# Keys split by half of the partitions, chunk 0 laid out tile by tile, and a new order of chunk 1's start

## The chip, the cores and the metric

The kernel runs on one core of a Trainium2 chip. A core has a tensor engine for matrix products (PE), a vector engine (DVE), a scalar engine for activation functions (ACT), a general engine that here mostly issues loads (GpSimd, POOL in the profile) and a queue engine (SP). Each works through its own instructions in order, and semaphores tie them together. Products land in PSUM, eight banks of 2 KB for each of 128 partitions; everything else lies in SBUF. The metric is the time of one execution on the device in microseconds; less is better.

## What is computed

Causal attention over 4 batches, 8 heads, 768 positions and head width 64, in which three heads (0, 2, 6) look at all earlier positions and the other five only at the first 4 positions (the sinks) and at the last 64. Its result, as a matrix of 3072 by 512, goes through two dense layers with a leaky ReLU between them:

```python
scores = scale * np.matmul(q, k.transpose(0, 1, 3, 2))
stream_keep = causal & (is_sink | in_win)
mask = np.where(retr[0, :, 0, 0, None, None], full_mask, stream_mask)
...
a = a / (np.sum(a, axis=-1, keepdims=True) + 1e-09)
...
h = x @ w_in
g = np.maximum(0.01 * h, h)
return (g @ w_out).astype(np.float32)
```

with `w_in` of 512 by 2048 and `w_out` of 2048 by 512.

## The kernel before

The 3072 rows are cut into eight chunks of 384 (a half of one batch's positions), worked on in the order batch 0 first half, batch 1 first half, batch 0 second half, and so on. Chunk n's attention gives x for that chunk (`xts[n]`), then come the first layer in 16 ticks (`in_slots`, lines 547 to 557: four matmuls of 384 columns each, then ACT's leaky ReLU) and the second (`out_slots`). From chunk 2 on, keys and queries are transposed by DMA, and attention of the next chunk is woven slot by slot into the dense layers of the present one. The schedule is written by hand: every engine's order is the order in which the code issues instructions.

The change touches the start, where nothing is there to weave with. Names that matter:

- `kt[i]` holds the keys of one batch, transposed: head width along partitions, two heads in one group of 128 partitions. For each head of a pair there is a copy in which the other half of the partitions is zero (index `hh`), so that a product over 128 partitions gives one head's scores. `move` with `hh` writes such a copy out of PSUM by multiplying with a column of zeros and ones (`half`), lines 184 to 193.
- Chunk 0 is handled in three tiles of 128 positions (`First(0)`, `First(1)`, `First(2)`, lines 445 to 541). `turn_tile` (line 209) transposes a tile's keys or queries on PE into a bank with tag `py` and empties it: keys' even half by DVE ("v"), odd half by ACT ("a"); queries by DVE. `all_heads` (469), `retr` (480) and `stream` (493) put a mask into a bank by an identity product, add scores, and have ACT take the exponential. `av` (504) multiplies with values, `finish` (529) divides on DVE, and `x_t` (537) turns the result on PE and copies it into `xts[0]`.
- `v_shift_pe` (152) makes values shifted by 64 positions (`vb`) by a product and a DVE cast (line 160). The windowed heads of tiles 1 and 2 need them.
- `in_tile(q4, j)` (559) does four first-layer ticks for one tile of chunk 0: 16 matmuls of 128 columns and one ACT instruction. `q4` 0 needs the first 512 columns of `w_in`, `q4` 1 the second.
- `turn_pair` (195) transposes chunk 1's keys or queries for one pair of heads. `zero_small`, `sink_keys` and `sink_values` prepare the sinks of a batch.
- `Attention(1).slots(order, lag)` (409) gives chunk 1's attention as 12 units (scores and exponential), each followed `lag` slots later by its product with the values, and three further slots for turning x. Its buffers are six for full heads and five for windowed heads.
- PSUM banks: two each of the tags `ph`, `psS`, `po` and `py`.
- Loads with a change of type are issued by GpSimd in program order (lines 617 to 638), onto one queue.

At the end of the start, the order is (lines 707 to 737): first-layer pieces of the first weights with the keys of chunk 1, DVE memsets, first-layer pieces of the second weights, the queries of chunk 1, sinks of batch 1, then chunk 1's attention, into which the ticks 8 to 15 of chunk 0 (`p0[8:]`) are merged.

Of the kernel before, what the change touches and what calls it, by code (L numbers as in the profile page):

```python
# [11 lines left out]
FP32 = mybir.dt.float32  # L12
# [5 lines left out]
CH = 384  # L18
# [3 lines left out]
def kernel(  # L22
# [59 lines left out]
    kt = [bf(f"kt{i}", 4, 2, S) for i in range(2)]  # L82
# [82 lines left out]
    def zero_keys(i, eng, lo, hi):  # L165
        for hh in range(2):
            eng.memset(kt[i][64 - 64 * hh : 128 - 64 * hh, :, hh, lo:hi], 0.0)
# [8 lines left out]
    def q_of(n, p, lo, hi):  # L176
        if n < 2:
            return qx[n][:, p, lo:hi]
        g = lo // 128
        if hi <= 128 * g + 128:  # L180
            return qx[n][:, g, p, lo - 128 * g : hi - 128 * g]
        return qx[n][:, g : hi // 128, p, :]
# [12 lines left out]
    def turn_pair(n, p, tags, engs, nms="kq"):  # L195
        b, c = ORDER[n]
        if n not in qx:
            qx[n] = rot.tile([128, 4, CH], BF16, name="qt", tag="qt", bufs=2)
        for nm, tag, eng in zip(nms, tags, engs):
            pt = bank(tag, [128, 4, 128], BF16)  # L200
            for g in range(3):
                nc.tensor.transpose(pt[:, g, :], raw[nm, n][:, g, 2 * p : 2 * p + 2, :], ident[:])
            if nm == "k":
                for hh in range(2):
                    move(eng, kt[b % 2][:, p, hh, CH * c : CH * c + CH].rearrange("p (g t) -> p g t", g=3), pt[:, 0:3, :], hh)
            else:
                move(eng, qx[n][:, p, :].rearrange("p (g t) -> p g t", g=3), pt[:, 0:3, :])

    def turn_tile(nm, j, engs, tag="py"):
        pt = bank(tag, [128, 4, 128], BF16)  # L210
        for p in range(4):
            nc.tensor.transpose(pt[:, p, :], (k0 if nm == "k" else q0)[:, j, 2 * p : 2 * p + 2, :], ident[:])  # L212
        t = slice(128 * j, 128 * j + 128)
        if nm == "q":
            move(engs, qx[0][:, :, t], pt[:])
        else:
            for hh in range(2):
                move(engs[hh], kt[0][:, :, hh, t], pt[:], hh)
# [8 lines left out]
    def spreads(n):  # L227
        b, c = ORDER[n]

        def spread(g, hh):  # L230
            r = slice(64 * hh, 64 * hh + 64)
            o = CH * c + 128 * g
            nc.vector.tensor_copy(kt[b % 2][r, :, hh, o : o + 128], raw["kx", n][r, g])  # L233

        r = [lambda g=g, hh=hh: spread(g, hh) for g in range(3) for hh in range(2)]
        if c == 0:
            r += sink_keys_by(b)
        return r
# [14 lines left out]
    def sink_keys_by(b):  # L253

        ks, kk = ksink[b % 2], kt[b % 2]

        def odd():
            nc.vector.tensor_copy(ks[64:128, :].rearrange("p (q t) -> p q t", t=SK)[:, :, NS : 2 * NS],
                                  kk[64:128, :, 1, 0:NS])

        def even():
            nc.vector.tensor_copy(ks[0:64, 256 + 4 * NS : 256 + 5 * NS], kk[0:64, 2, 0, 0:NS])

        return [odd, even]
# [9 lines left out]
    class Attention:  # L274
# [35 lines left out]
        def retr(self, h):  # L310
            p, hh = divmod(h, 2)
            i, c, n = self.i, self.c, self.n
            groups = [[(0, 0)], [(1, 128), (2, 256)]] if c == 0 else \
                [[(kj, 0)] for kj in range(4)] + [[(4, 128), (5, 256)]]
            r = []
            for grp in groups:
                box = {}

                def qk(grp=grp, box=box):
                    s = self.score()  # L320
                    a = rot.tile([128, CH], BF16, name="at", tag="at", bufs=6)
                    off = 0
                    for j, (kj, lo) in enumerate(grp):
                        w = CH - lo
                        nc.tensor.matmul(  # L325
                            s[:, off : off + w], lhsT=kt[i][:, p, hh, 128 * kj : 128 * kj + 128],
                            rhs=q_of(n, p, lo, CH), start=(j == 0), stop=(j == len(grp) - 1),
                            skip_group_check=True)
                        off += w
                    nc.scalar.activation(out=a[:, 0:off], in_=s[:, 0:off], func=ACTF.Exp, scale=SM)  # L330
                    if len(grp) == 2:
                        d = a.rearrange("p (j t) -> p j t", j=3)[:, 0:3:2, :]
                        nc.vector.tensor_mul(d, d, m_caus.rearrange("p (o t) -> p o t", o=1).to_broadcast([128, 2, 128]))  # L333
                    elif grp[0][0] >= 3 * c:
                        nc.vector.tensor_mul(a[:, 0:128], a[:, 0:128], m_caus[:])  # L335
                    box[0] = a

                def do_av(grp=grp, box=box):
                    off = 0
                    for (kj, lo) in grp:  # L340
                        for qi in range(lo // 128, 3):
                            o = off + 128 * qi - lo
                            self.av(p, hh, qi, box[0][:, o : o + 128], va[self.b][:, kj, h, :])
                        off += CH - lo

                r.append((qk, do_av, p))
            return r

        def stream(self, h):
# [4 lines left out]
            def qk():  # L354
# [3 lines left out]
                for m in range(6):  # L358
                    k0 = 64 * max(6 * c + m - 1, 0)
                    nc.tensor.matmul(  # L360
                        s[:, 64 * m : 64 * m + 64], lhsT=kt[i][:, p, hh, k0 : k0 + 128],
# [83 lines left out]
    class First:  # L445
        def __init__(self, j):
            self.j = j
            self.at_of, self.po, self.xs = {}, {}, {}
# [7 lines left out]
        def key(self, h, k0):  # L456
            return kt[0][:, h // 2, h % 2, k0 : k0 + 128]

        def query(self, h, lo=0, n=128):
            return qx[0][:, h // 2, 128 * self.j + lo : 128 * self.j + lo + n]  # L460
# [8 lines left out]
        def all_heads(self, half, tag):  # L469
            hs = (RETR + STREAM)[4 * half : 4 * half + 4]  # L470
            s = self.bank_with(tag, over(n_first, 4), 4) if half else bank(tag, [128, 4, 128], FP32)
            if not half:
                for x, m in ((slice(0, 3), over(n_caus, 3)), (slice(3, 4), over(n_first, 1))):
                    nc.tensor.matmul(s[:, x, :], lhsT=ident[:], rhs=m, start=(x.start == 0), stop=False, skip_group_check=True)
            for x, h in enumerate(hs):
                nc.tensor.matmul(s[:, x, :], lhsT=self.key(h, 0), rhs=self.query(h), start=False, stop=True,
                                 skip_group_check=True)
            nc.scalar.activation(out=self.at[:, 4 * half : 4 * half + 4, :], in_=s[:], func=ACTF.Exp, scale=SM)

        def retr(self, lo, hi, tag):  # L480
            s = self.bank_with(tag, over(n_caus, 3), 0 if lo else 3)
            for x, blk in enumerate(self.blocks[lo:hi]):
                if blk is None:
                    for p in range(4):
                        nc.tensor.matmul(s[:, x, :], lhsT=ksink[0][:, 128 * p : 128 * p + 128],
                                         rhs=qx[0][:, p, self.qs], start=(x == 0 and p == 0), stop=(p == 3),
# [17 lines left out]
        def av(self, half):  # L504
# [9 lines left out]
            for h in sorted(hs, key=lambda h: h not in RETR):  # L514
                x = h - 4 * half
                if j == 0:
                    mm(x, x + 1, self.at[:, (RETR + STREAM).index(h), :], va[0][:, 0, h, :])
# [19 lines left out]
        def x_t(self, tag, eng):  # L537
# [3 lines left out]
            move(eng, xts[0][:, :, self.qs], pt[:])  # L541
# [5 lines left out]
    def in_slots(n, tags=("ph",)):  # L547
        def tick(t):
# [3 lines left out]
            for g in range(KG):  # L552
                nc.tensor.matmul(ph[:, 0:CH], lhsT=w_in_bf[:, g, 128 * t : 128 * t + 128],  # L553
                                 rhs=xts[n][:, g, :], start=(g == 0), stop=(g == KG - 1))
# [4 lines left out]
    def in_tile(q4, j, tag="ph"):  # L559
# [3 lines left out]
        for x in range(4):  # L563
            t = 4 * q4 + x
            for g in range(KG):
                nc.tensor.matmul(ph[:, x, :], lhsT=w_in_bf[:, g, 128 * t : 128 * t + 128],  # L566
                                 rhs=xts[0][:, g, 128 * j : 128 * j + 128], start=(x == 0 and g == 0),
# [60 lines left out]
    load_qk(1, "k")  # L628
    load_in(512, 1024)
    load_qk(1, "q")  # L630
# [35 lines left out]
    qx[0] = rot.tile([128, 4, CH], BF16, name="qt", tag="qt", bufs=2)  # L666
    xts[0] = rot.tile([128, 4, CH], BF16, name="xt", tag="xt", bufs=2)
    F0, F1, F2 = (First(j) for j in range(3))
    idle("psS", 13)
    turn_tile("k", 0, "va")  # L670
    turn_tile("q", 0, "v")
    sink_values(0, nc.vector)
    nc.vector.tensor_copy(vs[0][0:32, :, D], m_sink[0:32, :])
    turn_tile("k", 1, "va")
    F0.all_heads(0, "psS")
    F0.all_heads(1, "ph")
    turn_tile("q", 1, "v")
    sink_keys(0)
    F1.retr(0, 4, "psS")
    F1.stream((1, 3, 4, 5), ats4[0], "ph")  # L680
    F0.av(0)
    F0.finish(0)
    turn_tile("k", 2, "va")
    F0.av(1)
    F1.retr(4, 7, "psS")
    F1.stream((7,), ats[0], "ph")
    turn_tile("q", 2, "v")
    F0.finish(1)
    v_shift_pe(0, "py", "v")
    F2.retr(0, 4, "psS")  # L690
    F2.retr(4, 8, "ph")
    F0.x_t("py", "v")
    F1.av(0)
    F1.finish(0)
    F2.stream((1, 3, 4, 5), ats4[1], "psS")
    nc.vector.memset(ats[1][:, :, 1:3, :], 0.0)
    F1.av(1)
    F1.finish(1)
    F2.retr(8, 10, "ph")
    F2.stream((7,), ats[1], "psS")  # L700
    v_shift_pe(1, "py", "v")
    F1.x_t("py", "a")
# [3 lines left out]
    F2.finish(1)  # L706
    in_tile(0, 0)
    in_tile(0, 1)
    F2.x_t("py", "v")
    turn_pair(1, 0, ("psS",), "v", "k")  # L710
    turn_pair(1, 1, ("psS",), "v", "k")
    in_tile(0, 2)
    turn_pair(1, 2, ("psS",), "v", "k")
    turn_pair(1, 3, ("py",), "v", "k")
# [4 lines left out]
    in_tile(1, 0)  # L719
    in_tile(1, 1)  # L720
    in_tile(1, 2)
# [5 lines left out]
    a1 = Attention(1, po_tags=("po", "po", "po", "py"), xt_eng="v").slots([0, 2, 6, 1, 3, 4, 5, 7], lag=4)  # L727
    sink_keys(1)
    sink_values(1, nc.vector)
    nc.vector.tensor_copy(vs[1][0:32, :, D], m_sink[0:32, :])  # L730


    run(a1[0:8])
    v_shift_pe(0, "ph", "v", 1)
    run(a1[8:9])
    v_shift_pe(1, "ph", "v", 1)
    run(a1[9:10], merge(p0[8:], a1[10:]))
# [76 lines left out]
```

## Time and profile before

| | |
|---|---|
| median of 13 runs | 239.71 us (238.51 to 242.73) |
| profiled execution | 238.64 us, of which the span from first to last instruction is 236.9 us |
| instructions | 5040 |
| granted clock of the tensor engine, mean | 1.0 |
| chunk 0's tiles, from the first turn (5.3 us) to the first-layer work (16.9 us) | 11.6 us |
| from there to chunk 1's first score (24.3 us) | 7.4 us |
| from there to the first tick of chunk 1's first layer (about 37.25 us) | 13.0 us |
| the rest | 199.6 us |

The page of the profile gives busy time by engine, the chain of work that ended last, and groups of instructions. The timeline lists instructions in order of time: start, duration, engine, line, operation, what is written from what, shape, and in brackets how long the engine had been idle and what released it. A row with "x6" merges six neighbours. The row of a matmul includes the time that the product takes to come out of the array, so neighbouring rows overlap; how far apart matmuls start is read from the next row's start. A transfer's "landing" counts from its issue.

### The profile page before, as it was taken

The page shows a single profiled execution, that of the slowest core. Times are in us where ns is not written, and L with a number is a line of the kernel's source. Part 1 is how long each engine was busy: PE and PEld are TensorE (multiplying, and loading weights), DVE is VectorE, ACT ScalarE, POOL GpSimd, SP SyncE. Part 2 cuts the span into 40 slices and gives each one's busy share as a digit, 9 for nine tenths or more (in the row PEclk, how much of TensorE's full clock was granted, in tenths as well). Part 3 has the DMA queues.
Part 4 walks back from the last instruction along what each step waited for, and adds up shares of the span by engine and source line. Part 5 has one row for each costly group of instructions (what it writes and reads, how often), then busy time and mean ns, then how long its engine had stood idle before and what let it go on. Part 6 is the DMA issues. An engine that isn't in the chain of part 4 may idle for free.

```text
span 236.9 us, 5040 instructions
## 1 busy us (share of the span) xinstructions
PE 225.1 (95%) x2029; PEld 139.2 (59%) x2057; DVE 98.6 (42%) x280; ACT 128.1 (54%) x276; POOL 69.9 (30%) x85
## 2 busy tenths in 40 slices
PE   5889899999999999999999999999999999999994
PEld 3679565545565666566556565666556665555553
DVE  6687777025356266446413651156212341111121
ACT  4565866623754888564356544765556763333300
POOL 8986525029075059009403900000000000000000
PEclk9999999999999999999999999999999999999999
DMA  9999999999999949999999992920210221111112
GB/s 129 159 184 163 206 207 163 177 113 173 168 248 203 215 79 134 167 134 122 142 131 193 160 146 61 225 75 17 78 47 0 64 69 26 47 44 44 47 44 90
DMA packets 109352, 28.98 MB, mean 122 GB/s; under 512 B 101264, under 2 KB 105616, under 8 KB 109328
## 3 DMA queue, kind: packets, MB, share of 16 engines
q0 software_dynamic: 77024, 13.37, 75.2%
q1 hardware_dynamic: 31248, 15.01, 29.1%
q10 hardware_dynamic: 1056, 0.26, 0.5%
q8 instruction: 16, 0.26, 0.4%
q14 instruction: 8, 0.07, 0.1%
HBM read 27.30 MB, written 6.29 MB: 142 GB/s over the span
## 4 chain that ended last, share of the span: by engine, by line
PE 87%; DVE 5%; ACT 3%; issue 2%; DMA 2%; POOL 0%; POOLq 0%; DVEq 0%
PE ph L553 32%; PE py L579 28%; PE po L294 6%; PE psS L325 5%; PE psS L579 4%; PE psS L360 2%; PE ph L566 2%; PE psS L305 2%; DMA out_dram<-o 2%; ACT ats L365 1%; PE psS L403 1%; PE py L212 1%; ACT at L330 1%; DVE xs L393 1%; PE po L510 1%
## 5 line engine op out<-in xcount | busy, mean ns | idle before, releaser
L553 PE MATMUL ph<-xt,w_in_bf 128*128 128x384 bf16 x480 | 95.5, 326 | 0.1
L555 ACT ACTIVATE g<-ph 128x384 bf16<-128x384 f32 x120 | 58.9, 491 | 57.8 <-PE ph L553 57.3
L579 PE MATMUL py<-w_out_bf,g 128*128 128x512 bf16 (+1 forms) x324 | 85.5, 374 | 1.4
L553 PEld LDWEIGHTS <-w_in_bf 128*128 128x128 bf16 x480 | 43.7, 97 | 31.3 <-issue 1.2
L579 PEld LDWEIGHTS <-g 128*128 128x128 bf16 x400 | 35.4, 97 | 25.9
L330 ACT ACTIVATE at<-psS 128x384 bf16<-128x384 f32 x78 | 36.9, 490 | 15.5 <-PE psS L325 15.3
L585 DVE COPY o<-py 128x512 f32<-128x512 f32 (+1 forms) x22 | 14.9, 678 | 51.8 <-PE py L579 50.4
L112 POOL DMA_DIRECT2D kb<-in_k_dram x21 | 18.7, 908 | 32.0 <-DMA kd<-kb 31.3
L325 PE MATMUL psS<-qd,kt 128*128 128x384 bf16 (+2 forms) x90 | 22.9, 293 | 0.0
L117 POOL DMA_DIRECT2D va<-in_v_dram x24 | 21.3, 911 | 2.5 <-DMA w_out_bf<-in_moe_w_out_dram 1.7
L112 POOL DMA_DIRECT2D qb<-in_q_dram x21 | 18.7, 917 | 4.7 <-DMA w_in_bf<-in_moe_w_in_dram 1.8
L294 PE MATMUL po<-va,at 128*128 128x65 bf16 x228 | 19.4, 193 | 0.3 <-DVE at L333 0.3
L365 ACT ACTIVATE ats<-psS 128x384 bf16<-128x384 f32 x35 | 17.0, 489 | 4.6 <-PE psS L360 4.2
L369 DVE TENSOR_TENSOR ats<-ats,m_win 128x384 bf16<-128x384 bf16 x35 | 13.0, 374 | 14.8 <-ACT ats L365 14.7
L294 PEld LDWEIGHTS <-at 128*128 128x128 bf16 x234 | 15.1, 98 | 5.6 <-DVE at L333 0.7
L393 DVE TENSOR_TENSOR xs<-po,linv 128x384 bf16<-128x384 f32 x27 | 15.1, 558 | 0.9
L335 DVE TENSOR_TENSOR at<-at,m_caus 128x128 bf16<-128x128 bf16 x21 | 4.7, 225 | 24.2 <-ACT at L330 24.1
L233 DVE COPY kt<-kd 64x512 bf16<-64x512 bf16 x36 | 14.4, 399 | 0.6
L360 PEld LDWEIGHTS <-kt 128*128 128x128 bf16 x210 | 10.8, 98 | 6.3 <-issue 0.4
L325 PEld LDWEIGHTS <-kt 128*128 128x128 bf16 x99 | 9.5, 97 | 7.7 <-issue 1.2
L294 PEld LDWEIGHTS <-ats 128*128 128x128 bf16 x210 | 10.0, 97 | 4.4 <-DVE ats L369 1.1
L333 DVE TENSOR_TENSOR at<-at,m_caus 128x256 bf16<-128x256 bf16 x21 | 6.1, 291 | 14.1 <-ACT at L330 14.1
(136 smaller groups left out, 192.8 us busy)
## 6 DMA issues: line engine op xcount, KB each, us to landing
out_dram<-o SPq DMA_DIRECT2D x23, 256.0 KB, 2.3
va<-in_v_dram POOLq DMA_DIRECT2D x24, 128.0 KB, 6.8
kb<-in_k_dram POOLq DMA_DIRECT2D x21, 128.0 KB, 5.5
qb<-in_q_dram POOLq DMA_DIRECT2D x21, 128.0 KB, 5.7
w_in_bf<-in_moe_w_in_dram POOLq DMA_DIRECT2D x4, 512.0 KB, 9.4
w_out_bf<-in_moe_w_out_dram POOLq DMA_DIRECT2D x4, 512.0 KB, 12.5
vb<-va SPq DMA_DIRECT2D x8, 195.0 KB, 4.0
vb<-va SPq DMA_DIRECT2D x4, 130.0 KB, 3.4
```

Source lines behind the costliest of these rows:

```text
L112: nc.gpsimd.dma_start(out=t[:, g], in_=nat[nm][b, c, :, :, g])
L117: nc.gpsimd.dma_start(out=va[b][:, 3 * c + g, :, 0:D], in_=nat["v"][b, c, :, :, g])
L294: nc.tensor.matmul(o, lhsT=lhsT, rhs=rhs, start=first, stop=False, skip_group_check=True)
L325: nc.tensor.matmul(s[:, off : off + w], lhsT=kt[i][:, p, hh, 128 * kj : 128 * kj + 128], rhs=q_of(n, p, lo, CH), start=(j == 0), stop=(j = ...
L330: nc.scalar.activation(out=a[:, 0:off], in_=s[:, 0:off], func=ACTF.Exp, scale=SM)
L360: nc.tensor.matmul(s[:, 64 * m : 64 * m + 64], lhsT=kt[i][:, p, hh, k0 : k0 + 128], rhs=q_of(n, p, 64 * m, 64 * m + 64), start=(m == 0), s ...
L365: nc.scalar.activation(out=av_, in_=s[:, 0:CH].rearrange("p (j e f) -> p j e f", j=3, e=2), func=ACTF.Exp, scale=SM)
L393: nc.vector.tensor_tensor(xs[:], po[:, :, :, 0:D], linv.to_broadcast([128, 3, 2, D]), op=ALU.mult)
L553: nc.tensor.matmul(ph[:, 0:CH], lhsT=w_in_bf[:, g, 128 * t : 128 * t + 128], rhs=xts[n][:, g, :], start=(g == 0), stop=(g == KG - 1))
L555: nc.scalar.activation(out=gs[n][:, t, :], in_=ph[:, 0:CH], func=ACTF.Prelu, alpha=0.01)
L579: nc.tensor.matmul(py[n][:, 0 : c1 - c0], lhsT=gs[n][:, ng, 128 * tt : 128 * tt + 128], rhs=w_out_bf[:, ng, c0:c1], start=(ng == 0), stop= ...
L585: nc.vector.tensor_copy(o[:, 0 : c1 - c0], py[n][:, 0 : c1 - c0])
```

## The change

Keys lie in one SBUF tile for each half of the partitions (`kt[i][hh]`), not in one tile with an index for it. Chunk 0's queries and x lie tile behind tile (`[128, 3, 4, 128]`), so each tile is written as one run, and the first layer reads x in three runs of 128. `turn_tile` is taken apart into `turn` (PE) and `empty` (DVE or ACT), and `all_heads` into `masked`, `all_heads` and `weigh`; the two groups of four heads in tile 0 become even heads (0, 2, 6, 4) and odd heads. `turn_pair` takes an engine for each half of the keys, DVE and ACT for chunk 1 where both were DVE. GpSimd issues chunk 1's queries ahead of the second 512 columns of `w_in`. The order of the start is rewritten, and in chunk 1 the products with values follow six slots behind their scores, not four.

```diff
-    kt = [bf(f"kt{i}", 4, 2, S) for i in range(2)]
+    kt = [[bf(f"kt{i}_{hh}", 4, S) for hh in range(2)] for i in range(2)]
...
-    def turn_tile(nm, j, engs, tag="py"):
-        pt = bank(tag, [128, 4, 128], BF16)
+    turned = {}
+
+    def turn(nm, j, tag="py"):
+        pt = turned[nm, j] = bank(tag, [128, 4, 128], BF16)
         for p in range(4):
             nc.tensor.transpose(pt[:, p, :], (k0 if nm == "k" else q0)[:, j, 2 * p : 2 * p + 2, :], ident[:])
-        t = slice(128 * j, 128 * j + 128)
+
+    def empty(nm, j, engs, hh=None):
+        pt = turned[nm, j]
         if nm == "q":
-            move(engs, qx[0][:, :, t], pt[:])
-        else:
-            for hh in range(2):
-                move(engs[hh], kt[0][:, :, hh, t], pt[:], hh)
+            move(engs, qx[0][:, j], pt[:])
+        for h, eng in zip(range(2) if hh is None else (hh,), engs if nm == "k" else ""):
+            move(eng, kt[0][h][:, :, 128 * j : 128 * j + 128], pt[:], h)
...
+        HEADS = (0, 2, 6, 4, 1, 3, 5, 7)
+
+        def masked(self, half, tag):
+            s = self.s[half] = self.bank_with(tag, over(n_first, 4), 4) if half else bank(tag, [128, 4, 128], FP32)
             if not half:
                 for x, m in ((slice(0, 3), over(n_caus, 3)), (slice(3, 4), over(n_first, 1))):
                     nc.tensor.matmul(s[:, x, :], lhsT=ident[:], rhs=m, start=(x.start == 0), stop=False, skip_group_check=True)
+
+        def all_heads(self, half):
+            hs, s = self.HEADS[4 * half : 4 * half + 4], self.s[half]
             for x, h in enumerate(hs):
                 nc.tensor.matmul(s[:, x, :], lhsT=self.key(h, 0), rhs=self.query(h), start=False, stop=True,
                                  skip_group_check=True)
-            nc.scalar.activation(out=self.at[:, 4 * half : 4 * half + 4, :], in_=s[:], func=ACTF.Exp, scale=SM)
+
+        def weigh(self, half):
+            nc.scalar.activation(out=self.at[:, 4 * half : 4 * half + 4, :], in_=self.s[half][:], func=ACTF.Exp, scale=SM)
...
-    load_qk(1, "k")
+    load_qk(1)
     load_in(512, 1024)
-    load_qk(1, "q")
     load_v(1)
...
     idle("psS", 13)
-    turn_tile("k", 0, "va")
-    turn_tile("q", 0, "v")
+    turn("k", 0)
+    empty("k", 0, "va")
+    turn("q", 0)
+    empty("q", 0, "v")
+    F0.masked(0, "psS")
+    F0.masked(1, "ph")
     sink_values(0, nc.vector)
+    turn("k", 1)
+    F0.all_heads(0)
+    F0.all_heads(1)
+    F0.weigh(0)
+    empty("k", 1, "va")
+    turn("q", 1)
+    empty("q", 1, "v")
+    F0.weigh(1)
+    sink_keys(0)
     nc.vector.tensor_copy(vs[0][0:32, :, D], m_sink[0:32, :])
-    turn_tile("k", 1, "va")
-    F0.all_heads(0, "psS")
-    F0.all_heads(1, "ph")
-    turn_tile("q", 1, "v")
-    sink_keys(0)
     F1.retr(0, 4, "psS")
     F1.stream((1, 3, 4, 5), ats4[0], "ph")
+    F1.retr(4, 7, "psS")
     F0.av(0)
+    turn("k", 2)
+    empty("k", 2, "v", 0)
     F0.finish(0)
-    turn_tile("k", 2, "va")
     F0.av(1)
-    F1.retr(4, 7, "psS")
+    empty("k", 2, "a", 1)
     F1.stream((7,), ats[0], "ph")
-    turn_tile("q", 2, "v")
+    turn("q", 2)
+    empty("q", 2, "v")
+    v_shift_pe(0, "py", "v")
     F0.finish(1)
-    v_shift_pe(0, "py", "v")
     F2.retr(0, 4, "psS")
     F2.retr(4, 8, "ph")
-    F0.x_t("py", "v")
     F1.av(0)
     F1.finish(0)
     F2.stream((1, 3, 4, 5), ats4[1], "psS")
+    F2.retr(8, 10, "ph")
+    F1.av(1)
+    F0.x_t("py", "v")
+    F1.finish(1)
     nc.vector.memset(ats[1][:, :, 1:3, :], 0.0)
-    F1.av(1)
-    F1.finish(1)
-    F2.retr(8, 10, "ph")
     F2.stream((7,), ats[1], "psS")
     v_shift_pe(1, "py", "v")
-    F1.x_t("py", "a")
     F2.av(0)
     F2.finish(0)
     F2.av(1)
     F2.finish(1)
+    F1.x_t("py", "a")
     in_tile(0, 0)
     in_tile(0, 1)
     F2.x_t("py", "v")
-    turn_pair(1, 0, ("psS",), "v", "k")
-    turn_pair(1, 1, ("psS",), "v", "k")
+    turn_pair(1, 0, ("psS",), ("va",), "k")
+    turn_pair(1, 1, ("psS",), ("va",), "k")
     in_tile(0, 2)
-    turn_pair(1, 2, ("psS",), "v", "k")
-    turn_pair(1, 3, ("py",), "v", "k")
+    turn_pair(1, 2, ("psS",), ("va",), "k")
+    turn_pair(1, 3, ("py",), ("va",), "k")
     nc.vector.tensor_copy(m_win0[:, 2:], m_one.rearrange("p (o t) -> p o t", o=1).to_broadcast([128, 4, 64]))
     zero_small(1, nc.vector)
     for a in ats[2:]:
         nc.vector.memset(a[:, :, 1:3, :], 0.0)
-    in_tile(1, 0)
-    in_tile(1, 1)
-    in_tile(1, 2)
+    sink_keys(1)
+    sink_values(1, nc.vector)
+    nc.vector.tensor_copy(vs[1][0:32, :, D], m_sink[0:32, :])
     turn_pair(1, 0, ("psS",), "v", "q")
     turn_pair(1, 1, ("py",), "a", "q")
     turn_pair(1, 2, ("psS",), "v", "q")
     turn_pair(1, 3, ("py",), "a", "q")
     p0 = in_slots(0)
-    a1 = Attention(1, po_tags=("po", "po", "po", "py"), xt_eng="v").slots([0, 2, 6, 1, 3, 4, 5, 7], lag=4)
-    sink_keys(1)
-    sink_values(1, nc.vector)
-    nc.vector.tensor_copy(vs[1][0:32, :, D], m_sink[0:32, :])
-
-
-    run(a1[0:8])
+    a1 = Attention(1, po_tags=("po", "po", "po", "py"), xt_eng="v").slots([0, 2, 6, 1, 3, 4, 5, 7], lag=6)
+
+
+    run(a1[0:3])
+    in_tile(1, 0)
+    run(a1[3:5])
+    in_tile(1, 1)
+    run(a1[5:6])
+    in_tile(1, 2)
+    run(a1[6:7])
     v_shift_pe(0, "ph", "v", 1)
-    run(a1[8:9])
+    run(a1[7:8])
     v_shift_pe(1, "ph", "v", 1)
-    run(a1[9:10], merge(p0[8:], a1[10:]))
+    run(a1[8:9], merge(p0[8:], a1[9:]))
```

## The prediction

> **What bounds the kernel now.** I read the page first (busy time, then the chain), then the waits, then the timeline of the first 38 us, where every edited line lies. On the page, the busy row (us, share of the span, instructions) and the chain's shares by engine:
>
> ```profile
> PE 225.1 (95%) x2029; PEld 139.2 (59%) x2057; DVE 98.6 (42%) x280; ACT 128.1 (54%) x276; POOL 69.9 (30%) x85
> ...
> PE 87%; DVE 5%; ACT 3%; issue 2%; DMA 2%; POOL 0%; POOLq 0%; DVEq 0%
> ```
>
> The tensor engine (PE) is the bound. After 38 us its waits that the profile names come to 1.2 us, so a shift made before 38 us goes through to the end almost whole. What can move is the start: chunk 0's tiles up to 16.9 us, then its first weights and chunk 1's turning up to 24.3, then chunk 1's attention. In the last of these (start:end, length, PE busy) the row is
>
> ```profile
> 24.28:37.25 12.97, 11.95 (x148) 1.00 1.32 202
> ```
>
> where PE has slack that busy time hides, since a matmul's row includes its pipeline. By start-to-start spacing (128 columns 0.056 us, 384 columns 0.163, 256 columns 0.109, 64 or 65 columns 0.03, two of 455 in 0.38) the content is: six score groups 0.98, sinks 0.44, 30 stream scores 0.84, 48 products with values 1.44, sink products 0.27, shifted values 0.77, 12 turns of x 0.67, eight first-layer ticks 8 x 0.65 = 5.2; together 10.6 of 12.97 us. So 2.4 us are open, 2.0 of them before the first tick at 29.73.
>
> **The start, part by part.** *Separate key tiles.* Among the waits between 5 and 25 us (total, times, longest) stands
>
> ```profile
> ACT kt L193 <- DVE kt L189: 2.2, 3, 1.0
> ```
>
> ScalarE (ACT) empties the odd half only when VectorE (DVE) has done the even one. Is the shared tile the reason, or the shared bank of PSUM? Two rows speak against the tile: DVE and ACT write chunk 1's query tile from two banks at once (DVE from 23.87 to 24.56, ACT from 24.19), and PE reads keys of tile 0 at 7.82 while DVE writes tile 1's until 8.11. The Trainium skill (PSUM — Partial Sum Buffer, "PSUM bank collisions raise a hardware error") speaks against this edit as well: two engines must be kept off one bank, two readers included. So I cost the split at zero. By the other reading all three waits would go; carried through the steps below, only 0.25 us of it reaches chunk 1, since DVE is late there anyway.
>
> *Masks ahead, even heads first.* Keys and queries of tile 0 are turned by 6.3; the masks' 1024 columns go out at the slow early rate (four 128-column matmuls in 0.43, in place of 0.22 after 9 us), 0.86 us, then tile 1's keys 0.43: first scores at 7.64, before 7.82. Tile 1's queries are then emptied at 9.20, before 9.41. Gain 0.2.
>
> *Tile 2's keys in two steps.* Shifted values need a bank ("py"). Turned at 10.78, the even half leaves on DVE at 11.21 (0.46 us). The odd half queues on ACT behind three exponentials (10.09, 10.57, 11.05) and waits for DVE: 11.74 to 12.43. The other bank holds tile 2's queries, on DVE behind the even keys and F0's division (0.55): free at 12.64. So the shift starts at 12.47, before 12.38: the gain is gone.
>
> *F0's x moved back.* These are DVE's rows around it before (start, duration, instruction):
>
> ```profile
> 13.80 0.42 DVE L187 COPY xt<-py 128x512 bf16<-128x512 bf16 x1 [0.20 <-PE py L540]
> 14.14 0.17 DVE L532 RECIPROCAL linv<-po 128x4 f32<-128x4 f32 x1
> 14.35 0.42 DVE L534 TENSOR_TENSOR xs<-po,linv 128x256 bf16<-128x256 f32 x1
> 14.76 0.22 DVE L696 MEMSET ats<- 128x192 uint32 x1
> 14.89 0.17 DVE L532 RECIPROCAL linv<-po 128x4 f32<-128x4 f32 x1
> 15.10 0.43 DVE L534 TENSOR_TENSOR xs<-po,linv 128x256 bf16<-128x256 f32 x1
> 15.66 0.63 DVE L160 CAST vb<-py 128x455 bf16<-128x455 f32 x1
> ```
>
> The copy filled a gap at 13.80. Now it comes after F1's second product: PE turns x at 14.94, DVE copies at 15.37 (0.34 to the next), then division 0.55 and memset 0.2, and the cast of shifted values, on which F2's products wait, starts at 16.47 in place of 15.66: 0.8 later. F1's x is no longer turned inside that wait but after it, 4 x 0.056 = 0.22. Chunk 0's first-layer work then starts at 17.9, before 16.89: **+1.0**. Not shown in any row is how the engines fall into step in the new order. Ends: -0.2 if the copy finds a gap again, +1.3 if each stall is paid in full; I take +1.0, the rows above it in sequence.
>
> **Chunk 1's queries.** Before, DVE's queue there was:
>
> ```profile
> 19.10 0.42 DVE L187 COPY xt<-py 128x512 bf16<-128x512 bf16 x1 [1.18 <-PE py L540]
> 19.44 2.16 DVE L189 TENSOR_SCALAR kt<-psS,half 128x384 bf16<-128x384 bf16 x6
> 21.51 0.73 DVE L189 TENSOR_SCALAR kt<-py,half 128x384 bf16<-128x384 bf16 x2
> 22.16 0.22 DVE L715 COPY m_win<-m_one 128x256 bf16<-128x256 bf16 x1
> 22.38 0.28 DVE L170 MEMSET ksink<- 128x272 uint32 x1
> 22.73 0.49 DVE L171 MEMSET vs<- 128x520 bf16 x1
> 23.21 0.63 DVE L718 MEMSET ats<- 128x192 uint32 x3
> 23.87 0.69 DVE L187 COPY qt<-psS 128x384 bf16<-128x384 bf16 x2
> 24.59 0.58 DVE L258 COPY ksink<-kt 64x16 bf16<-64x16 bf16 x1
> 25.19 0.16 DVE L262 COPY ksink<-kt 64x4 bf16<-64x4 bf16 x1
> 25.26 0.61 DVE L127 TENSOR_TENSOR vs<-vsf,m_sink 32x448 bf16<-32x448 f32 x1
> 25.80 0.28 DVE L730 COPY vs<-m_sink 32x8 bf16<-32x8 bf16 x1
> ```
>
> It is full from 19.10 to 26. PE spent 20.82 to 23.5 on the second weights (48 matmuls, 2.69 us), which covered this list; the queries' copy at 23.87 came just as they were turned. The change takes that cover away and moves the last four rows ahead of the queries. Anew, from x at 19.10 + 1.0 = 20.1: x 0.34, two even key halves 0.72, to 21.17. The other two wait until PE, which may begin the third tile of the first weights only after x (20.58, 0.9 us), has turned keys again: 21.85, to 22.57. Window mask and memsets, 22.16 to 23.87 before: 1.71, to 24.28. Sink keys and values 1.5, to 25.75. First query copy 0.35; **first score at 26.15, before 24.28: +1.85, of it 0.85 from here**. ACT takes the four odd halves; of 128x384 with a scale there is no row, the nearest are ACT's plain copy (0.44) and its 128x512 with scale (0.69). I take 0.5: done by 23.4, under DVE's list; at 0.69 by 24.2, still under it. Ends for this part: 0.5 if DVE's small rows shrink (sink keys took 0.28 the first time, 0.58 here), 1.1.
>
> *Transfers.* GpSimd issued the second weights at 10.91 (landing 9.1 us later) and chunk 1's queries from 11.65 (9.1 each). Exchanged, the queries land some 2.7 us sooner, near 19.9, and the weights near 22.6 (2.7 is the time from chunk 1's last keys, 17.3, to these weights, 20.0). Needed at 22.0 and 27.2: nothing waits, nothing is gained, because DVE's list decides. At their old place, 20.8, these weights would cost 1.8. What GpSimd issues next (values, third weights) keeps its place; SP issues nothing in the moved steps.
>
> **Chunk 1's attention** now holds 10.6 + 2.7 = 13.3 us of content. The weight pieces fill part of the 2.0 us that waited for exponentials; the first scores still wait for banks and ACT. I leave 0.9 us open: 14.2, before 12.97: **+1.2**. Ends: +0.7 (only the 0.35 behind 29.73 stays open) and +2.7 (nothing filled). Lag 6 only lets products wait longer; the six score buffers and five stream buffers are just enough. The matmul that reads x with a stride of 512 has a near row: chunk 2's scores read queries so, at 0.33 us like the others: zero.
>
> **Sum:** 1.0 + 0.85 + 1.2 = 3.05. The profiled execution took 238.64 (span 236.9), so 241.7 by its own time. It was among the quickest; the median is 239.71, and I carry the same 3.0 there: **242.7 us**. Ends: 239.71 + (-0.2 + 0.5 + 0.7) = 240.7, and + 5.1 = 244.8.
>
> **Rivals.** *Clock drop, slower still.* Between 21.8 and 26.15 PE would have only 12 transposes, 0.67 us of work. The skill (TensorE: Matmul & The Clock Gate, "HAM oscillation — how this bites in real kernels") says that an idle window of about 3.4 us halves the clock. In this trace no pause after 9 us is longer than 0.6, so no row shows it; what half rate costs, its first 9 us show (four turns in 0.61, later 0.39). By the row: nothing. By the rule: some 3.4 us at half rate lose 1.7: 244.4. Whether turns count as work is open; chance 0.25.
> *Faster: DVE's list ends early.* It is four key halves shorter (1.44 us), and the start may tighten more than I think. If the first query copy came at 21.6, right behind its turn, the score would follow at 22.0, and 22.0 + 14.2 = 36.2 against 37.25: 238.7. It decides below 23.0 for the first score; above, the 14.2 eats it. Against it: five groups of rows stand ahead of that copy in DVE's order. Chance 0.12.
> *No change:* the start gains 0.8 in place of losing 1.0 and attention loses only 0.7: 239.71 - 0.8 + 0.85 + 0.7 = 240.4, near the edge of no change. Chance 0.07, shared by same and slower.
>
> **The numbers.** My forecast has 0.56. About 0.3% (0.7 us) is what a measurement of this kernel can tell from no change. Faster 0.12, same 0.05, slower 0.83. Range 240.7 to 245.0: both ends of the sum and the clock drop are inside, the fast case and most of the even one are out, under 2 in 10.
>
> **What would show it.** ACT's odd keys still 0.04 behind DVE's; the cast of shifted values for F2 near 16.5; DVE's first copy of chunk 1's queries near 25.7, with PE nearly empty for 4 us ahead; the last turn of chunk 1's x followed by chunk 1's ticks near 40.2. Wrong if that copy comes before 23, if odd and even keys overlap, or if weight matmuls after the pause run at 0.11 us each.

## The result, and the profile after

The changed kernel takes **242.81 us**, median of 11 runs (241.37 to 243.0); the kernel before, run on the same chips, 239.89 us (48 runs). The ratio is 1.0106, with a 95% interval of 1.0082 to 1.0129: slower by 2.9 us. The forecast was 242.7. Its sum is right and its composition is not: a cost that it put at nothing was made good by others that it had too large, so part of the hit is luck. The rest of this text is about the difference. Runs named e1 to e12 are the experiments below.

The profiled execution took 241.56 us (span 239.8). The 11 times fall into two groups, four near 241.5 and seven from 242.3 to 243.0; the profile is of the first, and what parts the two is open. From its page, the busy row, the granted TensorE clock in 40 slices, and the chain's shares by engine:

```profile
PE 225.1 (94%) x2029; PEld 139.5 (58%) x2057; DVE 96.4 (40%) x276; ACT 129.7 (54%) x280; POOL 70.0 (29%) x85
...
PEclk9999799999999999999999999999999999999999
...
PE 88%; DVE 3%; ACT 3%; DMA 2%; issue 1%; ACTq 0%; DVEq 0%
```

PE is as busy as before to the tenth, 225.1 us, in a span that is 2.9 longer. The one digit that differs from a 9 is the fifth slice, 24 to 30 us: there the clock was cut. The windows of that stretch (start:end length, then PE, PEld, DVE, ACT, POOL busy, clock, DMA share, GB/s) cover chunk 1's key and query turning, the first 7.9 us of its attention, and the rest of it:

```profile
20.78:24.42 3.64, 1.15 (x13) 0.79 (x12) 3.55 (x14) 2.27 (x5) 1.29 (x3) 1.00 2.05 174
24.42:32.28 7.86, 7.54 (x96) 6.39 (x96) 2.68 (x10) 5.22 (x12) 3.97 (x5) 0.78 1.24 205
32.28:40.17 7.89, 7.89 (x106) 5.45 (x103) 5.99 (x19) 4.83 (x11) 3.64 (x5) 1.00 1.83 181
```

For 3.64 us PE worked 1.15, and DVE 3.55. Then comes a stretch at a mean clock of 0.78; the trace's own record has half rate from 24.98 to 28.39, 3.41 us long. What PE waited for up to 41 us, the costliest first (total, times, longest):

```profile
PE psS L328 <- DVE qt L187: 1.9, 1, 1.9
PE py L214 <- DVE k L671: 1.3, 1, 1.3
PE po L519 <- DVE vb L160: 1.1, 1, 1.1
PE py L156 <- ACT kt L193: 0.6, 1, 0.6
```

The first is new: chunk 1's first score waits 1.9 us for DVE to copy the queries. This is DVE's queue ahead of that copy (start, duration, instruction):

```profile
18.89 0.42 DVE L187 COPY xt<-py 128x512 bf16<-128x512 bf16 x1 [1.40 <-PE py L549]
19.23 0.73 DVE L189 TENSOR_SCALAR kt<-psS,half 128x384 bf16<-128x384 bf16 x2
20.67 0.42 DVE L189 TENSOR_SCALAR kt<-psS,half 128x384 bf16<-128x384 bf16 x1 [0.71 <-PE psS L202]
...
21.33 0.22 DVE L734 COPY m_win<-m_one 128x256 bf16<-128x256 bf16 x1
...
23.02 0.31 DVE L261 COPY ksink<-kt 64x16 bf16<-64x16 bf16 x1
23.35 0.16 DVE L265 COPY ksink<-kt 64x4 bf16<-64x4 bf16 x1
23.42 0.61 DVE L127 TENSOR_TENSOR vs<-vsf,m_sink 32x448 bf16<-32x448 f32 x1
23.96 0.17 DVE L740 COPY vs<-m_sink 32x8 bf16<-32x8 bf16 x1
24.03 0.60 DVE L187 COPY qt<-psS 128x384 bf16<-128x384 bf16 x2
```

The queries had been turned by 22.6; mask and memsets hold DVE until 23.02, and from there to 24.03 the sinks' four rows alone hold the copy. And PE's rows from there on:

```profile
22.23 0.33 PE L202 MATMUL py<-ident,qb 128*128 128x128 bf16 x3
24.42 0.59 PE L328 MATMUL psS<-qt,kt 128*128 128x384 bf16 x3 [1.87 <-DVE qt L187]
25.32 0.48 PE L328 MATMUL psS<-qt,kt 128*128 128x384 bf16 x1 [0.31 <-ACT at L333]
25.60 1.91 PE L575 MATMUL ph<-xt,w_in_bf 128*128 128x128 bf16 x16
27.30 0.84 PE L328 MATMUL psS<-qt,kt 128*128 128x256 bf16 x3
27.95 1.27 PE L575 MATMUL ph<-xt,w_in_bf 128*128 128x128 bf16 x16
```

The first weight piece takes 1.70 us from start to start (25.60 to 27.30), 0.106 a matmul; 16 such matmuls at full clock take 0.9, as the first experiment below shows.

To see where the time arises, three points of each profile are enough: the start of chunk 0's first-layer work, chunk 1's first score, and the start of the ticks behind chunk 1's last turn of x ("last ticks"). A column "later by" gives the time since the point to its left. From the last point to the end it is 200.3 us in the kernel before and after, and within 0.3 of it in most experiments, so what is lost up to it is what is lost. The last column belongs to the start: PE's clock is half in the first microseconds and rises at a time that differs from execution to execution.

| kernel (profile) | first-layer work | first score | later by | last ticks | later by | full clock from |
|---|---|---|---|---|---|---|
| before | 16.89 | 24.28 | 7.39 | 36.60 | 12.32 | 8.86 |
| after | 16.68 | 24.42 | 7.74 | 39.53 | 15.11 | 4.50 |
| e1, pause filled | 17.98 | 25.58 | 7.60 | 39.22 | 13.64 | 9.90 |
| e3, weights back | 17.43 | 25.17 | 7.74 | 37.56 | 12.39 | 8.21 |
| e9, queries first | 17.73 | 23.44 | 5.71 | 37.32 | 13.88 | 8.82 |
| e11, before with a longer warm-up | 16.01 | 23.39 | 7.38 | 35.72 | 12.33 | 6.84 |

Between the two kernels nearly the whole loss lies in chunk 1's attention, 15.11 against 12.32.

### The profile page after: what moved, and what is told of

Read it like the earlier page. It is cut to its first block, busy times and chain, and to the rows that moved or that the text cites. A ratio compares the mean times of both kernels' runs of the same rounds, so it can differ in the third digit from the quotient of the medians.

```text
span 239.8 us, 5042 instructions
## 1 busy us (share of the span) xinstructions
PE 225.1 (94%) x2029; PEld 139.5 (58%) x2057; DVE 96.4 (40%) x276; ACT 129.7 (54%) x280; POOL 70.0 (29%) x85
## 3 DMA queue, kind: packets, MB, share of 16 engines
HBM read 27.30 MB, written 6.29 MB: 140 GB/s over the span
## 4 chain that ended last, share of the span: by engine, by line
PE 88%; DVE 3%; ACT 3%; DMA 2%; issue 1%; ACTq 0%; DVEq 0%
PE ph L562 32%; PE py L588 30%; PE po L297 7%; PE psS L328 6%; PE psS L588 4%; PE ph L575 3%; PE psS L363 3%; DMA o<-in_q_dram 2%; PE psS L308 2%; PE psS L406 1%; ACT ats L368 1%; PE po L519 1%; ACT at L333 1%; ACT kt L193 1%; ACT at L487 0%
## 5 line engine op out<-in xcount | busy, mean ns | idle before, releaser
L372 DVE TENSOR_TENSOR ats<-ats,m_win 128x384 bf16<-128x384 bf16 x35 | 12.5, 361 | 15.3 <-ACT ats L368 14.9
L236 DVE COPY kt<-kd 64x512 bf16<-64x512 bf16 x36 | 13.4, 371 | 0.6
```

## The experiments

Each was timed in five rounds beside the kernel before. Ratios are to that kernel, with 95% intervals.

| run | median us | ratio | interval |
|---|---|---|---|
| after | 242.81 | 1.0106 | 1.0082 to 1.0129 |
| e1_filled_pause | 241.18 | 1.0044 | 1.0025 to 1.0064 |
| e2_sinks_behind | 240.56 | 1.0034 | 1.0013 to 1.0055 |
| e3_weights_back | 240.33 | 1.0026 | 1.0007 to 1.0045 |
| e4_weights_back_load_late | 241.04 | 1.0052 | 1.0031 to 1.0072 |
| e5_x_turned_early | 242.18 | 1.0102 | 1.0065 to 1.0139 |
| e6_layouts_alone | 239.64 | 0.9993 | 0.9965 to 1.0021 |
| e7_load_order_alone | 240.96 | 1.0055 | 1.0026 to 1.0084 |
| e8_put_together | 240.15 | 1.0025 | 1.0000 to 1.0049 |
| e9_queries_first | 239.86 | 1.0015 | 0.9994 to 1.0035 |
| e10_queries_first_old_load | 240.59 | 1.0021 | 0.9998 to 1.0045 |
| e11_before_warm | 239.76 | 0.9997 | 0.9977 to 1.0017 |
| e12_queries_first_warm | 240.05 | 1.0013 | 0.9990 to 1.0035 |

### Filling the pause: what the clock costs

```diff
     turn_pair(1, 3, ("py",), "a", "q")
+    idle("ph", 16)
```

Sixteen matmuls on a blank tile stand behind the last query turn; their sums are overwritten, so only PE's idleness goes.

> The changed kernel with 16 matmuls of 256 columns on zeros (1.75 us of work) on the tensor engine behind the last turn of chunk 1's queries, where it stood empty for some 1.9 us. Theory A (the pause lets the clock fall to half for 3.4 us, and that costs about 1.5 us): granted clock 1.0 throughout, each weight piece of chunk 1's attention 0.9 us, first score still at 24.4, 241.3 us, 1.3 to 1.7 under the changed kernel. Theory B (half rate falls where the tensor engine waits for exponentials anyway, the loss is the moved work itself): no more than 0.4 under the changed kernel, 242.4 or more.

Measured: 241.18 us, 1.6 less than after, by adding work. In 21 of 22 runs the mean clock stayed at 0.995 or more; in all 12 runs of the changed kernel on record it was 0.992 or 0.993. (Such a mean doesn't say where the drop lies; the kernel before has one in 18 of the 75 runs beside these.) PE's rows of this kernel, whose profile has no drop:

```profile
23.69 1.91 PE L150 MATMUL ph<-blank 128*128 128x256 bf16 x16
25.58 0.59 PE L328 MATMUL psS<-qt,kt 128*128 128x384 bf16 x3
26.48 0.32 PE L328 MATMUL psS<-qt,kt 128*128 128x384 bf16 x1 [0.31 <-ACT at L333]
26.64 1.05 PE L575 MATMUL ph<-xt,w_in_bf 128*128 128x128 bf16 x16
27.53 0.49 PE L328 MATMUL psS<-qt,kt 128*128 128x256 bf16 x3
```

The same weight piece now takes 0.89 us from start to start (26.64 to 27.53), and attention up to the last ticks 13.64 in place of 15.11. So the drop is caused by the pause and costs about 1.5 us (1.47 by the profiles, 1.6 by the medians). The +1.3 that is left against before's 12.32 is the moved weight work itself, as e3 below shows.

### The sinks behind the queries

```diff
-    sink_keys(1)
-    sink_values(1, nc.vector)
-    nc.vector.tensor_copy(vs[1][0:32, :, D], m_sink[0:32, :])
     turn_pair(1, 0, ("psS",), "v", "q")
 ...
     turn_pair(1, 3, ("py",), "a", "q")
+    sink_keys(1)
+    sink_values(1, nc.vector)
+    nc.vector.tensor_copy(vs[1][0:32, :, D], m_sink[0:32, :])
```

> The changed kernel with the sinks of batch 1 (keys, values, mask column) behind the emptying of chunk 1's queries on VectorE, not ahead of it. Theory A (VectorE's list ahead of the queries sets the first score): first score 1.0 us sooner, at 23.4; the emptiest stretch of the tensor engine shrinks by as much, so the clock may or may not fall: 241.8 if it falls, 240.3 if it doesn't. Theory B (the first score is set by turning or by the queries' arrival): first score at 24.4, 242.8.

Measured: 240.56 us. The first score comes 6.59 us after the first-layer work in place of 7.74, and PE's wait for the query copy is 0.7 instead of 1.9. That is 1.15 for four rows that occupy DVE 1.0: what stands ahead of the copy is paid in full. The shorter pause also leaves the clock alone in some runs: in 10 of 22 the mean clock is 0.993 (median 241.45), in 12 near 1.0 (median 240.45).

### The second weights back ahead of the queries

```diff
-    load_qk(1)
+    load_qk(1, "k")
     load_in(512, 1024)
+    load_qk(1, "q")
 ...
+    in_tile(1, 0)
+    in_tile(1, 1)
+    in_tile(1, 2)
     turn_pair(1, 0, ("psS",), "v", "q")
```

The three `in_tile(1, ·)` among chunk 1's slots are gone; sinks stay ahead of the queries. The second kernel, e4, makes the same change but keeps the changed load order.

> The changed kernel with the second weights' three pieces back between keys and queries of chunk 1, and their load ahead of the queries' again. Theory A (the moved pieces were the cover of VectorE's list; without them pause, clock and less overlap cost all that was lost): clock 1.0, first score at 24.3 to 24.5, first tick of chunk 1's first layer near 37.3, time 239.8, within 0.4 of the kernel before. Theory B (lag 6, keys emptied on two engines or sinks ahead cost on their own): 240.6 or more.

> As the third, but the load of the second weights stays behind the queries'. Theory A (the queue moves its data in order, so these weights land near 22.3 where 20.7 is needed): the tensor engine waits some 1.6 us at the first of the three pieces and the time is 1.3 to 1.7 over the third. Theory B (the order on the queue is of no account): same as the third.

Measured: 240.33 and 241.04. With the weights back, attention is 12.39 (before 12.32), with the first score at the same 7.74 after the first-layer work as in after: the moved work made nothing earlier there, and against e1 its place in attention costs 1.25 less 0.14 by the profiles, 0.85 by the medians. DVE's list is covered by the weight matmuls again. No clock drop is in e3's profile, and its mean clock is under 0.995 in 6 of 22 runs, about as often as in the kernel before. The late load costs 0.7 by the medians, half of what was expected. In e4's own profile the first-layer work began late (18.20), and the weights were nearly there when they were needed; that executions with an earlier start pay more was not seen, only argued.

### The opening: x turned where before turned it

```diff
     F2.retr(4, 8, "ph")
+    F0.x_t("py", "v")
     F1.av(0)
 ...
     F1.av(1)
-    F0.x_t("py", "v")
     F1.finish(1)
 ...
     v_shift_pe(1, "py", "v")
+    F1.x_t("py", "a")
     F2.av(0)
 ...
-    F1.x_t("py", "a")
     in_tile(0, 0)
```

> The changed kernel with the turning of F0's and F1's x at the places that it has in the kernel before (F0's ahead of F1's products, F1's ahead of F2's). Theory A (the x copy and the division behind it hold up VectorE's cast of shifted values): the tensor engine's wait for that cast shrinks from 1.1 to about 0.4 us, and F1's turn (0.2) goes into it; first-layer work of chunk 0 starts 0.7 to 0.9 sooner against the start of the first shift of values. Of that, the pause in front of chunk 1's first score lets through all: 241.9 to 242.1. Theory B (the cast waits for its product or the products for exponentials): no change, 242.6 to 242.9.

Measured: 242.18 us in six runs, not to be told from after, and the first-layer work begins at 16.68 in both, with the clock full from 4.2 and 4.5. The wait shrank as Theory A said, but the time that it promised didn't come. PE's waits up to 25 us show why:

```profile
PE py L549 <- DVE xs L543: 0.6, 1, 0.6
...
PE po L519 <- DVE vb L160: 0.2, 1, 0.2
```

The wait for the cast of shifted values fell from 1.1 to 0.2, but the turn now waits 0.6 for its input, which DVE delivers later in the new order. One edit alone doesn't take the loss back.

### The layouts alone, and the load order alone

The first is the kernel before with the changed tiles only (keys in a tile for each half, chunk 0's queries and x in one run for each tile):

```diff
-    kt = [bf(f"kt{i}", 4, 2, S) for i in range(2)]
+    kt = [[bf(f"kt{i}_{hh}", 4, S) for hh in range(2)] for i in range(2)]
 ...
-                move(engs[hh], kt[0][:, :, hh, t], pt[:], hh)
+                move(engs[hh], kt[0][hh][:, :, t], pt[:], hh)
```

The second is the kernel before with `load_qk(1)` ahead of `load_in(512, 1024)`.

> The kernel before with the layouts of the changed one alone (keys in a tile for each half, queries and x of chunk 0 tile behind tile) and its own order. Theory A (ScalarE waits for VectorE because both read one bank): its waits for even keys stay at three and about 2.2 us in total, time as before within 0.3. Theory B (they wait because both write one tile): no such wait, tile 0's odd keys at 6.0 in place of 6.5, and up to 0.3 us less time.

> The kernel before with chunk 1's queries loaded ahead of the second weights, its order otherwise untouched. Theory A (data moves in the order of the queue): these weights land near 22.3 in place of 20.0, the first piece that needs them waits 0.8 to 1.5 us, 240.8 to 241.3. Theory B: no change, 239.9.

Measured: 239.64 and 240.96. ACT's waits up to 17 us in the first:

```profile
ACT kt L193 <- DVE kt L189: 1.8, 3, 0.9
```

Three waits are still there (2.2 before) although the halves lie in two tiles. So the shared tile was not what made ACT wait. What the two engines still share is the bank that they read; that it is the reason is inferred, since no run gave them two banks. In the second kernel PE's timeline has

```profile
23.28 2.85 PE L566 MATMUL ph<-xt,w_in_bf 128*128 128x128 bf16 x48 [1.06 <-DMA w_in_bf<-in_moe_w_in_dram]
```

The weights come 1.1 late at their old place, and the median rises by as much. (The mean clock is under 0.995 in 11 of its 20 runs against 16 of 49 of before, so a part of the rise may be clock.) The exchange of loads is free only where the weights are wanted later.

### Everything that helped, together

After, with e3's and e2's edits, x turned early as in e5, and the first shift of values in the bank "ph":

```diff
-    v_shift_pe(0, "py", "v")
+    v_shift_pe(0, "ph", "v")
     F0.finish(1)
```

> Put together: the changed kernel's opening up to tile 2, the first shift of values in a bank of tag ph in place of py (so it needn't wait for tile 2's odd keys), x turned early, second weights and their load back, sinks behind the queries. Theory A (each of these is worth what its own run shows): first-layer work of chunk 0 near 16.5 where the clock rises as late as in the profile of before (16.9 there), no pause, 239.2, under the kernel before by 0.5 to 0.9. Theory B (the opening gains nothing that lasts): 239.9 or more.

Measured: 240.15 us. It isn't ahead of the kernel before, nor to be told from e3: the opening gives no gain in any form that was tried.

### Chunk 1's queries ahead of DVE's list

```diff
     turn_pair(1, 3, ("py",), ("va",), "k")
+    turn_pair(1, 0, ("psS",), "v", "q")
+    turn_pair(1, 1, ("py",), "a", "q")
+    turn_pair(1, 2, ("psS",), "v", "q")
+    turn_pair(1, 3, ("py",), "a", "q")
     nc.vector.tensor_copy(m_win0[:, 2:], ...)
 ...
-    turn_pair(1, 0, ("psS",), "v", "q")
-    turn_pair(1, 1, ("py",), "a", "q")
-    turn_pair(1, 2, ("psS",), "v", "q")
-    turn_pair(1, 3, ("py",), "a", "q")
```

The window mask, memsets and sinks follow the queries; e10 is the same with the load order of before.

> The changed kernel with chunk 1's queries emptied on VectorE right behind the keys: window mask, memsets and sinks of batch 1 come after them. Theory A (VectorE's list is what stands ahead of the first score, and the weight pieces fit into the waits of chunk 1's attention): first score near 21.8, no pause over 1 us, clock full from there on, 238.4, which is 1.2 to 1.8 under the kernel before. Theory B (something else, such as the masks behind the list or ScalarE's exponentials, takes its place): 239.8 or more.

> As the kernel with queries emptied first, but the second weights are loaded ahead of the queries, as before. Theory A (queries then land near 22.5, where their turning could start at 20.7): the tensor engine waits for them 1 to 2 us, the time is 0.8 to 1.6 over that kernel. Theory B: same.

Measured: 239.86 and 240.59. DVE's rows of the first:

```profile
22.06 0.41 DVE L189 TENSOR_SCALAR kt<-py,half 128x384 bf16<-128x384 bf16 x1
22.38 0.35 DVE L187 COPY qt<-psS 128x384 bf16<-128x384 bf16 x1
23.17 0.36 DVE L187 COPY qt<-psS 128x384 bf16<-128x384 bf16 x1 [0.44 <-PE psS L202]
23.45 0.26 DVE L738 COPY m_win<-m_one 128x256 bf16<-128x256 bf16 x1
```

The copy now follows the keys, and the first score comes 5.71 after the first-layer work: 1.7 sooner than before and 2.0 sooner than after. Its profile has no clock drop. So the moved weights could be paid for, nearly: -1.7 at the queries, +1.6 in attention (13.88), +0.8 in the opening. It ends where before ends, not at the 238.4 expected. With the old load order PE waits for the queries themselves:

```profile
PE psS L202 <- DMA qb<-in_q_dram: 1.8, 3, 0.6
```

and the clock falls again (25.60 to 29.02 in its profile). By the medians the new load order is worth 0.7 here, but the two intervals overlap almost wholly, so only the wait is shown and not its worth.

The profile of e9 has the clock full from 8.82, as before had (8.86), and shows the opening at like clock. DVE's rows:

```profile
15.25 0.42 DVE L187 COPY xt<-py 128x512 bf16<-128x512 bf16 x1 [0.62 <-PE py L549]
...
16.21 0.22 DVE L718 MEMSET ats<- 128x192 uint32 x1
16.35 0.57 DVE L160 CAST vb<-py 128x455 bf16<-128x455 f32 x1
```

and PE's:

```profile
14.83 0.38 PE L549 MATMUL py<-ident,xs 128*128 128x128 bf16 x4
...
16.97 0.19 PE L519 MATMUL po<-vb,ats 128*128 128x65 bf16 x1 [1.07 <-DVE vb L160]
...
17.51 0.38 PE L549 MATMUL py<-ident,xs 128*128 128x128 bf16 x4
17.73 1.45 PE L575 MATMUL ph<-xt,w_in_bf 128*128 128x128 bf16 x23
```

The prediction had 14.94, 15.37, 16.47 and 17.9 for the turn, the copy, the cast and the first-layer work; here they are 14.83, 15.25, 16.35 and 17.73. The products wait 1.07 for the cast (0.30 before), and F1's turn follows at 17.51 with its 0.22.

### A longer warm-up

```diff
-    idle("psS", 13)
+    idle("psS", 19)
```

on the kernel before (e11) and on e9 (e12).

> The kernel before with 19 in place of 13 matmuls on zeros at the start, so that the tensor engine is busy until about 5.1 us and not 3.8. Theory A (the clock rises with the first fixed window of 3.4 us that is busy enough, and the hole from 4.0 to 5.3 spoils one in many runs): it is full by 8 us at the latest, the median falls by 0.3 to 0.7, to 239.2 to 239.6. Theory B (the rise doesn't depend on that hole): 239.9, rise between 4 and 12.4 us.

> Queries emptied first and 19 matmuls on zeros. Theory A: both gains add, 237.8 to 238.2. Theory B (the opening is held by VectorE and ScalarE[...]): as with queries emptied first alone.

Measured: 239.76 and 240.05, both no change. Yet in e11's profile chunk 1's last ticks start at 35.72, 0.9 ahead of before. In this profile the lead is lost near 70 us. DVE and PE there:

```profile
70.10 0.69 DVE L585 COPY o<-py 128x512 f32<-128x512 f32 x1 [3.08 <-DMA out_dram<-o]
```

```profile
71.55 0.39 PE L403 MATMUL psS<-ident,xs 128*128 128x128 bf16 x3 [2.18 <-DVE xs L393]
```

DVE's output copy waits 3.1 us until a store has emptied its buffer, PE waits 2.2 behind it, and the clock is at half from 71.7 to 75.1. In before the same copy waits 1.1 and PE 0.2. Three buffers take turns here, so the store waited for must be one of the two that SP issued at 63.76 and 64.39, behind two transposing loads; stores of this stretch land 5.1 to 5.5 us after their issue. No run moved them. The profile of e12, from its slowest execution, has the same pause (DVE 4.0, PE 3.1, half rate from 74.4). But 18 of 22 runs of e11 have a mean clock of 0.995 or more, so such a drop isn't what holds most of them; the medians say only that nothing is gained, and why is open.

## Why the prediction was right, and where it was not

**The total** (+3.05 forecast, +2.9 measured) is right, in part by luck. By medians it splits into 1.6 for the clock (after less e1), forecast as nothing; 0.85 for the weights' new place at full clock (e1 less e3), forecast as 1.2; and 0.4 for what e3 still has against before, the opening and the queries, forecast as 1.85. By profiles it is 0.84 for the opening, 0.35, 1.32 and 1.5 below, of which 1.05 is hidden in the changed kernel's profile, because its clock rose early.

**The opening, +1.0:** the chain of steps is right, row by row, as e9 shows: +0.84 at like clock. In the changed kernel's own profile the first-layer work starts 0.2 earlier than before, but that execution had full clock from 4.50 us and not from 8.86. From the first shift of values on, both have it. PE's first shift and first-layer work, before and after:

```profile
12.38 0.55 PE L156 MATMUL py<-va,shift 128*128 128x455 bf16 x2 [0.52 <-DVE qt L187]
16.89 1.28 PE L566 MATMUL ph<-xt,w_in_bf 128*128 128x128 bf16 x20
...
11.27 0.55 PE L156 MATMUL py<-va,shift 128*128 128x455 bf16 x2 [0.59 <-ACT kt L193]
16.68 1.50 PE L575 MATMUL ph<-xt,w_in_bf 128*128 128x128 bf16 x24
```

That is 4.51 and 5.41; the forecast had 5.43 (12.47 to 17.9). It is 4.50 or 4.51 in all four profiles with before's order and 5.40 or 5.41 in all eight with the changed one. What the prediction didn't see is that the x turn isn't the only cause: put back, it waits for its own input, and it stays 5.43 (e5). The medians give less: e3, which by its points has +0.84, +0.35 and +0.07, is 0.4 above before (interval 0.2 to 1.1). Before's profiled execution was 1.1 to 1.3 quicker than its medians (239.71 and 239.89) and e3's 0.5, so profiles and medians can't be set against each other more closely; where the rest lies is open.

**Chunk 1's queries, +0.85:** mis-sized; the profile has +0.35 (7.74 against 7.39). The order and the waiting are as forecast: the third key half starts 1.78 after the x copy (1.75 forecast), mask and memsets take 1.69 (1.71). The term that failed is the sinks' 1.5 us, taken from rows where they stood in another place; they took 1.01.

**Chunk 1's attention, +1.2:** right at full clock by the profile, +1.32 in e1, 13.64 against 12.32 (0.85 by the medians). In the changed kernel it is +2.8, because of the next point.

**The clock at nothing:** this is the step that failed. The prediction priced the clock drop as a rival of chance 0.25, by the rule in the Trainium skill (TensorE: Matmul & The Clock Gate, "HAM oscillation — how this bites in real kernels"), at 1.7, and left it out of its sum. It came: the mean clock is lowered in every run, at a cost of 1.5 to 1.6. The sign of being wrong that the prediction named, weight matmuls after the pause at 0.11 us each, came true as well (0.106). The rule speaks of gaps without work of about 3.4 us. Here the longest gap was 1.87 us, in a stretch of 3.64 with 1.15 of turning in it, and the clock fell all the same. The turns didn't keep it up. The total stayed under the rival's 244.4 only because the other terms came out smaller by the medians.

**The parts at zero:** the split key tile is zero (e6), and ACT's four odd halves hide under DVE's list (done at 22.17; each 0.57, estimated 0.5). The load exchange costs nothing in the changed order as far as its trace shows, where nothing waits for these loads; no run put the old load order there. With the weights at their old place it costs (e4, e7).

**The fast rival** asked for the query copy right behind its turn. DVE's order forbade it, as the prediction argued; where the order was changed (e9), the score came 1.7 sooner and attention took it back, so even then it was 239.86 and not 238.7.

## What to carry to other kernels

Work on the bound engine that seems movable may be the cover of another engine's list: before moving it, list what that engine still has ahead of the next thing the bound engine needs, and move that list first. A stretch with little matmul work can be paid twice, once as a wait and once in the clock after it, and sixteen matmuls on a blank tile can be cheaper than the pause. A gain at the start can be lost again at the next buffer that must come free, as in e11's profile.

## What the runs showed that was not expected

The time at which the clock first becomes full is not a property of the kernel: with the same 13 warm-up matmuls it lies between 3.9 and 12.2 us in the profiles of these runs, and the first-layer work follows it. Two of them (e6, e8) were at full clock near 4 us and then at half again, 7.5 to 10.9 and 7.3 to 10.7. Each such drop lasted 3.41 us, those after 20 us too. So a lead or a lag of a microsecond in a single profile's opening is no evidence about a kernel until the clock's rise stands beside it.

The drops also keep to a grid. In all eight profiles with a drop inside the program it begins a whole number of steps of 3.41 us behind the first rise (after: 4.50 + 6 x 3.413 = 24.98; e10: 8.54 + 5 x 3.413 = 25.60; e11: 6.84 + 19 x 3.413 = 71.69). Three single steps, of 3.41 us each:

| kernel (profile) | step | PE busy | behind it |
|---|---|---|---|
| after | 21.57 to 24.98 | 1.21 | half rate |
| e2 | 21.54 to 24.96 | 1.76 | half rate |
| e9 | 22.47 to 25.88 | 2.30 | full clock |

In the step ahead of each of the eight drops PE's rows cover 1.1 to 1.8 us; the emptiest step at full clock without a drop behind it has 2.2, but for one of 1.6 near the end of e7. So in these traces it was not the length of one gap that counted but how full such a step was, and since the grid lies otherwise in each execution, a shorter pause as in e2 meets it only in some. This is read from the traces; no run moved the grid.
